# A fused linear-attention and MLP block, rewritten on a list scheduler with the output projection folded into the KV product

## The chip, the cores and the metric

The kernel runs on one core of a Trainium2 chip. The metric is device time in microseconds (us). Several executions of each kernel are timed, and kernels that are compared ran on the same chip beside fresh executions of the kernel before. Each execution also lists its span, which is the length that the trace shows, and the mean clock that the throttle granted to TensorE. An execution that lies more than 1.5% above the fastest of its kernel is called slow.

PE is TensorE's matmul pipe, PEld its weight loads, DVE is VectorE, ACT is ScalarE, POOL is GpSimd, SP is the engine that issues most loads.

## The reference, cut to what matters

```python
S, D, F, H = 2048, 448, 1792, 16              # Dh = 28, bfloat16
xn  = layernorm(x)
q, k, v = split(xn @ wqkv)                    # 3 x 448 columns
phi = lambda t: where(t > 0, t + 1, exp(t)) + 1e-6
kv  = einsum("bhsd,bhse->bhde", phi(k), v);  z = phi(k).sum(over s)
o   = (phi(q) @ kv) / (phi(q) . z + 1e-6)     # per head
s   = o @ wo
g   = silu(relu(xn @ w1 + b1) ** 2 @ w2 + b2)
out = x + s * g
```

The 2048 tokens are 16 tiles of 128, handled as four groups of four tiles. D = 448 is contracted in four chunks of 112 rows, in both kernels.

## The kernel before

It is written engine by engine, with semaphores set by hand. For each group it emits K, V and Q per tile, then the 14 blocks of W1. After the last group come the KV product, the denominators, and a phase that interleaves W2 with the attention output. Here are the parts that the change and the argument touch.

The start: 64 dummy matmuls, the transposes of group 0, 24 more dummies, then K and V. The bias b1 comes in a column layout, element by element, from GpSimd's queue.

```python
emit("pe", pe_prewarm(64))
for piece in ln_pieces(0):
    for fpc in piece:
        emit("dve", fpc)
emit("pe", pe_transposes(0))
emit("pe", pe_prewarm(24))
# ... in GpSimd's setup:
with nc.allow_non_contiguous_dma(reason="b1 column layout"):
    e.dma_start(b1f[:, :], B_b1.rearrange("(fi p) -> p fi", p=P)).then_inc(s_b1, 16)
# ... on SP: x as four single tiles, then the weights
for j in range(min(4, NT)):
    e.dma_start(x_tok[:, j : j + 1, :], x_r[:, j : j + 1, :]).then_inc(s_x0[j], 16)
e.dma_start(w_qkv[:PD, :, :], A_wqkv.rearrange("(c p) j -> p c j", p=PD)).then_inc(s_wqkv, 16)
```

The denominators (16 matmuls, each using 16 columns of the array), the 16 spreads of 1/den over the rows of a head, and the 16 numerator steps:

```python
# pe_denhs(ni), for each of four groups:
for c in range(NC_D):
    last = e.matmul(DHps[ni][:NH, 0:512], zind[:PD, c, :], pqT[:PD, c, ni * 512 : (ni + 1) * 512],
                    start=(c == 0), stop=(c == NC_D - 1))
# pe_rdb(w), one bank per (group, chunk):
e.matmul(RBps[w % 2][:PD, 0:512], ehead[:NH, c, :], r16[:NH, ni * 512 : (ni + 1) * 512], start=True, stop=True)
# pe_numT(w):
e.matmul(OBps[w % 2][:PD, 0:512], kvbd[:PD, c, :], pqT[:PD, c, ni * 512 : (ni + 1) * 512], start=True, stop=True)
# ... ScalarE copies it to xoT; pe_s(si) multiplies it with w_o, four matmuls per tile
```

## Time and profile before

| | us |
|---|---|
| time, median of three | 183.68 (183.58 to 183.89) |
| span of the profiled execution | 183.8 |
| first K matmul | 11.51 |
| W1 of group 0 begins | 21.03 |
| group 1 begins | 37.25 |
| denominators end, first W2 tile begins | 113.21 |
| last W2 tile ends, after it the last four matmuls | 177.9, 178.7 |

These lines are from the profile page of the kernel before: the busy time of the engines with its share of the span, the granted TensorE clock in 40 slices (in tenths), and the chain of waits by engine and by line.

```profile
PE 171.7 (93%) x968; PEld 89.5 (49%) x968; DVE 126.0 (69%) x294; ACT 96.8 (53%) x156; POOL 27.2 (15%) x42
...
PEclk9999999999999999999999999999999999999997
...
PE 75%; DMA 10%; DVE 7%; POOL 2%; issue 2%; ACT 1%; POOLq 0%; DVEq 0%; ACTq 0%
PE pb L715 24%; PE pb L549 19%; DMA b1f<-in_B_b_dram 10%; PE pb L757 6%; PE pb L468 6%; PE pb L438 5%; PE pb L450 5%; PE pb L667 3%; PE pb L691 2%; PE pb L633 2%; DVE r2hT L573 2%; PE pb L597 2%; DVE xn_tok L342 2%; PE pb L401 1%; ACT ra L5
```

PE is busy for 93% of the span, so only matmuls that go away, or a shorter start and tail, can save much. The load of b1 is 10% of the chain. Next, PE's timeline of the kernel before. The columns are start and length in us, engine and line, operation and operands with their shape, count, and in brackets the idle time just before and what ended it.

```profile
1.59 6.37 PE L824 MATMUL pb<-ident 128*128 128x128 bf16 x64 [1.59 <-POOL eps L218]
...
8.75 1.50 PE L824 MATMUL pb<-ident 128*128 128x128 bf16 x24
11.51 0.93 PE L438 MATMUL pb<-w_qkv,xoT 112*128 112x448 bf16 x4 [1.26 <-DMA w_qkv<-in_A_wqkv_dram]
...
21.03 3.62 PE L549 MATMUL pb<-xoT,w 112*128 112x512 bf16 x16
26.00 6.20 PE L549 MATMUL pb<-xoT,w 112*128 112x512 bf16 x28 [1.35 <-ACT ra L563]
...
109.66 3.62 PE L633 MATMUL pb<-pqT,zind 112*16 112x512 bf16 x16 [0.44 <-DVE zind L611]
...
121.83 0.38 PE L691 MATMUL pb<-pqT,kvbd 112*112 112x512 bf16 x1
122.14 0.42 PE L667 MATMUL pb<-r_50,ehead 16*112 16x512 bf16 x1
122.50 2.82 PE L715 MATMUL pb<-w,r2hT 128*128 128x448 bf16 x14
```

K waits for its weights. In the first W1 stage PE stops for 1.35 us on ScalarE's relu, which itself waits for b1: that load takes 19 us. The lines from 109.66 to 122.14 us are the small attention matmuls. A spread costs a slot of 0.36 us (122.14 to the next matmul at 122.50), a numerator 0.31, and the denominators 3.62 us together.

### The profile page before, as it was taken

Reading aid. Unit: us, or ns where it says so; the run is one execution under the profiler, and the core shown is the slowest. Engines: PE = TensorE matmul, PEld = TensorE weight load, DVE = VectorE, ACT = ScalarE, POOL = GpSimd, SP = SyncE. Lnnn points to the kernel's source line nnn. Section 1 sums busy time; section 2 is a strip of 40 time slices with the busy share of each in tenths; the row PEclk is TensorE's granted clock in tenths of the full one; section 3 lists DMA queues with packets and bytes.
Section 4 is the critical chain, followed back from the end, with each engine's and each line's share of the span. In section 5 each row is a group of like instructions: output and inputs, shape, how many; then the busy total and the mean of one; then the engine's idle time right before and its main releaser. Section 6 shows DMA issues by size and latency. Waiting matters only on the chain.

```text
span 183.8 us, 2904 instructions
## 1 busy us (share of the span) xinstructions
PE 171.7 (93%) x968; PEld 89.5 (49%) x968; DVE 126.0 (69%) x294; ACT 96.8 (53%) x156; POOL 27.2 (15%) x42
## 2 busy tenths in 40 slices
PE   6979979799998999989999999999999999999980
PEld 6945424455444554445544474444444444434540
DVE  3727959969999699996995440194665556587454
ACT  6447557477784777748778747932332222352120
POOL 7500000000000000000000000000015544468320
PEclk9999999999999999999999999999999999999997
DMA  5999990000000000000000000000000000112101
GB/s 119 258 264 230 253 334 21 0 5 0 0 0 4 0 0 0 2 4 0 0 0 4 2 0 4 0 0 0 0 0 29 27 25 30 45 50 79 50 26 49
DMA packets 9629, 8.78 MB, mean 48 GB/s; under 512 B 2256, under 2 KB 8720, under 8 KB 9616
## 3 DMA queue, kind: packets, MB, share of 16 engines
q1 hardware_dynamic: 7808, 8.60, 17.4%
q0 software_dynamic: 1808, 0.01, 1.4%
q8 instruction: 8, 0.13, 0.3%
q14 instruction: 5, 0.04, 0.1%
HBM read 6.77 MB, written 1.84 MB: 47 GB/s over the span
## 4 chain that ended last, share of the span: by engine, by line
PE 75%; DMA 10%; DVE 7%; POOL 2%; issue 2%; ACT 1%; POOLq 0%; DVEq 0%; ACTq 0%
PE pb L715 24%; PE pb L549 19%; DMA b1f<-in_B_b_dram 10%; PE pb L757 6%; PE pb L468 6%; PE pb L438 5%; PE pb L450 5%; PE pb L667 3%; PE pb L691 2%; PE pb L633 2%; DVE r2hT L573 2%; PE pb L597 2%; DVE xn_tok L342 2%; PE pb L401 1%; ACT ra L563 1%
## 5 line engine op out<-in xcount | busy, mean ns | idle before, releaser
L549 PE MATMUL pb<-xoT,w 112*128 112x512 bf16 x224 | 49.7, 379 | 1.4 <-ACT ra L563 1.4
L563 ACT ACTIVATE ra<-pb,b1f 128x512 bf16<-128x512 f32 x56 | 37.7, 688 | 19.0 <-PE pb L549 14.6
L715 PE MATMUL pb<-w,r2hT 128*128 128x448 bf16 x224 | 45.0, 353 | 0.0
L800 POOL TENSOR_TENSOR outb<-tt_52,x_tok 128x448 bf16<-128x448 f32 x15 | 21.2, 1417 | 149.6 <-DVE tt_52 L788 149.6
L549 PEld LDWEIGHTS pb<-xoT,w 112*128 112x128 bf16 x224 | 21.7, 98 | 27.2 <-issue 1.8
L715 PEld LDWEIGHTS pb<-w,r2hT 128*128 128x128 bf16 x224 | 20.9, 98 | 21.4 <-issue 3.1
L737 ACT ACTIVATE sgm_54<-gb_53 128x448 bf16<-128x448 bf16 x16 | 9.2, 576 | 39.9 <-DVE gb_53 L728 39.9
L573 DVE TENSOR_TENSOR r2hT<-ra 128x512 bf16<-128x512 bf16 x56 | 22.0, 422 | 8.6 <-ACT ra L563 8.6
L728 DVE TENSOR_TENSOR gb_53<-pb,b2b 128x448 bf16<-128x448 f32 x16 | 10.0, 624 | 23.3 <-PE pb L715 23.3
L468 PE MATMUL pb<-xoT,w_qkv 112*112 112x512 bf16 x64 | 16.4, 379 | 0.0
L438 PE MATMUL pb<-w_qkv,xoT 112*128 112x448 bf16 x64 | 14.7, 353 | 1.3 <-DMA w_qkv<-in_A_wqkv_dram 1.3
L450 PE MATMUL pb<-w_qkv,xoT 112*128 112x448 bf16 x64 | 14.7, 352 | 0.0
L757 PE MATMUL pb<-w_o,xoT 112*128 112x448 bf16 x64 | 14.7, 352 | 0.0
L503 DVE TENSOR_SCALAR rt_q<-pb 112x512 bf16<-112x512 f32 x16 | 11.1, 691 | 4.2 <-ACT e_q L487 4.2
L768 DVE TENSOR_TENSOR gg_51<-gb_53,sgm_54 128x448 f32<-128x448 bf16 x16 | 10.0, 624 | 4.7 <-ACT sgm_54 L737 4.6
L788 DVE TENSOR_TENSOR tt_52<-pb,gg_51 128x448 f32<-128x448 f32 x16 | 10.0, 625 | 4.2 <-PE pb L757 3.8
L494 DVE TENSOR_SCALAR rt_k<-pb 128x448 bf16<-128x448 f32 x16 | 10.0, 625 | 3.9 <-ACT e_k L479 3.3
L487 ACT ACTIVATE e_q<-pb 112x512 bf16<-112x512 f32 x16 | 9.6, 597 | 5.1 <-PE pb L468 5.1
L479 ACT ACTIVATE e_k<-pb 128x448 bf16<-128x448 f32 x16 | 8.7, 544 | 4.4 <-PE pb L438 4.4
L517 DVE SCALAR_TENSOR_TENSOR pqT<-e_q,rt_q 112x512 bf16<-112x512 bf16 x16 | 11.0, 685 | 0.0
L699 ACT ACTIVATE xoT<-pb 112x512 bf16<-112x512 f32 x16 | 9.3, 585 | 3.0 <-PE pb L691 3.0
L468 PEld LDWEIGHTS pb<-xoT,w_qkv 112*112 112x112 bf16 x64 | 8.3, 130 | 5.2
(65 smaller groups left out, 153.6 us busy)
## 6 DMA issues: line engine op xcount, KB each, us to landing
w<-in_B_w_dram SPq DMA_DIRECT2D x2, 1568.0 KB, 15.8
out_dram<-outb SPq DMA_DIRECT2D x16, 112.0 KB, 1.7
x_tok<-in_A_x_dram SPq DMA_DIRECT2D x3, 448.0 KB, 17.4
w_qkv<-in_A_wqkv_dram SPq DMA_DIRECT2D x1, 1176.0 KB, 8.8
x_tok<-in_A_x_dram SPq DMA_DIRECT2D x4, 112.0 KB, 2.1
w_o<-in_A_wo_dram SPq DMA_DIRECT2D x1, 392.0 KB, 19.8
b2b<-in_B_b_dram SPq DMA_DIRECT2D x1, 112.0 KB, 13.5
b1f<-in_B_b_dram POOLq DMA_DIRECT2D x1, 7.0 KB, 19.0
```

The costliest lines, as they stand in the source:

```text
L438: last = e.matmul(Kps[:, 0:D], xoT[:PD, c, si * 128 : (si + 1) * 128], w_qkv[:PD, c, QW : QW + D], start=(c == 0), stop=(c == NC_D - 1),)
L450: last = e.matmul(Vps[:, 0:D], xoT[:PD, c, si * 128 : (si + 1) * 128], w_qkv[:PD, c, VW : VW + D], start=(c == 0), stop=(c == NC_D - 1),)
L468: last = e.matmul(Qps[t % 2][:PD, 0:512], w_qkv[:PD, c, m * PD : (m + 1) * PD], xoT[:PD, c, g * 512 : (g + 1) * 512], start=(c == 0), stop ...
L494: e.tensor_scalar(out=rt_k[:, si % 2, :], in0=Kps[:, 0:D], scalar1=0.0, scalar2=1e-6, op0=ALU.max, op1=ALU.add,).then_inc(sv_rtk, 1)
L503: e.tensor_scalar(out=rt_q[:PD, t % 2, :], in0=Qps[t % 2][:PD, 0:512], scalar1=0.0, scalar2=1e-6, op0=ALU.max, op1=ALU.add,).then_inc(sv_r ...
L517: e.scalar_tensor_tensor(out=pqT[:PD, m, g * 512 : (g + 1) * 512], in0=e_q[:PD, t % 2, :], scalar=1.0, in1=rt_q[:PD, t % 2, :], op0=ALU.mi ...
L549: last = e.matmul(pb[bk][:, 0:512], w_1[:PD, c, fi * 128 : (fi + 1) * 128], xoT[:PD, c, g * 512 : (g + 1) * 512], start=(c == 0), stop=(c ...
L563: e.activation(out=ra[:, u % NRB, :], in_=pb[h_bank(fi)][:, 0:512], func=AF.Relu, bias=b1f[:, fi : fi + 1],).then_inc(sa_hr, 1)
L573: e.tensor_tensor(out=r2hT[:, fi, g * 512 : (g + 1) * 512], in0=ra[:, u % NRB, :], in1=ra[:, u % NRB, :], op=ALU.mult,).then_inc(sv_sq, 1)
L715: last = e.matmul(Gps[si % NGD][:, 0:D], r2hT[:, fi, si * 128 : (si + 1) * 128], w_2[:, fi, :], start=(fi == 0), stop=(fi == NF - 1),)
L757: last = e.matmul(Sps[si % 2][:, 0:D], xoT[:PD, c, si * 128 : (si + 1) * 128], w_o[:PD, c, :], start=(c == 0), stop=(c == NC_D - 1),)
L800: e.tensor_tensor(out=outb[:, si % 3, :], in0=tt[:, si % 2, :], in1=x_tok[:, si, :], op=ALU.add,).then_inc(sm_, 1)
```

## The change

The intent: describe the work as operations with reads and writes, let a list scheduler with assumed durations fix the order of each engine (the orders of PE and of the load queue stay as written), and shorten PE's stream on the way. The core of the diff is this:

```diff
-        emit("pe", pe_prewarm(64))
-        emit("pe", pe_transposes(0))
-        emit("pe", pe_prewarm(24))
+        warm(40)
+        pe_transpose([0])
...  (group 0: one transpose and one K/V pair per tile, in turn)
+                kv(0)
+                for si in range(1, 4):
+                    pe_transpose([si])
+                    kv(si)
...  (loads)
-            for j in range(min(4, NT)):
-                e.dma_start(x_tok[:, j : j + 1, :], x_r[:, j : j + 1, :]).then_inc(s_x0[j], 16)
+        load_x(0, 1)
+        load_k("act", w_qkv, A_wqkv, "wqkv", 3 * D)
+        load_x(1, 4)
+        dma("sp", b1r[:, :], B_b1.rearrange("(f p) -> f p", p=P), ["b1r"], F * 2)
...  (Wo folded into the masked KV block; z comes out of the same bank)
-                e.matmul(OBps[w % 2][:PD, 0:512], kvbd[:PD, c, :], pqT[...], start=True, stop=True)
+                e.matmul(ps(b)[0:PD, 0:D], kvm[0:PD, c, :], w_o[0:PD, c, :], start=True, stop=True)
+                return e.matmul(ps(b)[0:PD, D : D + 32], kvm[0:KA, c, :], zsel[0:KA, c, :], start=True, stop=True)
...  (denominators: group g in columns 32g to 32g+31 of one bank)
+                for c in range(4):
+                    for g in range(NG):
+                        last = e.matmul(
+                            ps(denb)[32 * g : 32 * g + 32, 0:512], msb[0:PD, c, D : D + 32],
+                            pqT[0:PD, c, g * 512 : (g + 1) * 512], start=(c == 0), stop=(c == 3),
+                        )
...  (spread: four groups from four 32-row strips)
+                for g in range(NG):
+                    r = slice(32 * g, 32 * g + 32)
+                    last = e.matmul(ps(bufs[g])[0:PD, 0:512], ehd[r, c, :], rden[r, :], start=True, stop=True)
```

The rest of the diff: phi is computed in place, the gate is one Silu in place of Sigmoid and a multiplication, 1/sqrt comes from a power on GpSimd, and b1 arrives as 14 rows that PE transposes. A constant `SPLIT64` could lay the fourth chunk out as two 64-row halves that run side by side; it is `False`, so 4 x 112 rows remain.

## The prediction

> **What bounds it now.** The 183.68 us are a TensorE stream. In the chain of waits PE holds 75%, and from about 34 us it is unbroken. The chain's timeline gives the issue spacing: 0.216 us per 512-column matmul (W1: 12 in 2.59 us), 0.189 per 448-column one (4 in 0.756). Summed over K, V, Q, W1, W2, Wo, the transposes and the small attention matmuls, that is about 162 us of the 166.4 between the first QKV matmul (11.51 us, waiting for w_qkv) and the last (177.9). Lost outside the stream: 11.5 us of start; about 3.5 us in the first W1 stage (24.65 to 26.0 idle for b1, which lands at 25.17, then transposes waiting for VectorE); 5.8 us of tail.
>
> **What goes.** (1) The numerator matmuls disappear because Wo is folded into KV: 16 steps of 0.22 to 0.35 us, about 4.0. (2) Denominators (16 matmuls, 3.62 us) go to four 32-column groups, and the 1/den spreads (16 steps of 0.35, and each makes the next W2 run 0.10 longer: 2.75 against 2.65 us, together about 7 us) to four 32-row groups. The build gives them distinct array tiles. The Trainium skill ("TensorE: Matmul & The Clock Gate", Part 3) reports about 3x for four row tiles at once; no trace here shows it yet. Estimate: 1.0 us and 4 x 0.6. (3) The b1 wait. (4) Sigmoid times gate (10 us of VectorE): off the critical path. (5) The tail: one VectorE multiply, one SBUF add of about 0.4 us each for two tiles, then the store: about 4.0.
>
> **What comes.** Four fold steps, about 1.0 us. After the denominators Ln, a table load (1.28 us in the trace) and Exp no longer hide behind two W2 tiles, only one: about 1.1 us of PE idle.
>
> PE stream: 162 - 4.0 - 2.6 - 4.6 + 1.0 = about 152 us.
>
> **The start gets worse, I think.** w_qkv now shares the DMA engines with x from a second queue; the same bytes moved at about 260 GB/s in the old trace, so it lands near 11.3 us as before. Only 40 warm-up matmuls run (to about 6 us), so the first K/V probably run at half clock (same page, Part 1). And the static VectorE order puts the statistics of x tile 8 before the evacuation of transposed tile 3. Those x tiles landed at 21.6 us in the old trace, after the same 4.2 MB; I expect about 20. So PE stalls 2 to 3 us before tile 3's K/V. W1 of group 0 starts near 26 us (before: 21.0), group 1 near 39 (before: 37.4).
>
> **Sum.** 39 + two groups of 23.2 + last group with fold and denominators 24.8 = 110.3 (old end of denominators: 113.3). Then 16 W2 tiles x 2.65, 16 output tiles x 0.756, spreads 2.4, idle 1.1, small losses 0.3: 168.3. Tail 4.0: about 172 us, 6.4% less. Range 168 to 176.5.
>
> **Right or wrong, step by step.** Den group about 1 us and each spread about 0.6 in the timeline, else add up to 5 us. PE idle before the first spread naming ScalarE. VectorE waiting for the x load in the first 22 us, with PE idle behind it. Groups 1 and 2 at 23 us each with no PE idle over 0.3 us. W2 at 2.65 us throughout.
>
> **What would break it.** Row or column groups running one after another (175 to 177). A static order that makes PE wait for VectorE in every group. A faster x load (168 to 169).

## The result, and the profile after

| | before | after |
|---|---|---|
| time, median | 183.78 (183.58 to 184.96, 4 executions) | 176.69 (174.86 to 178.96, 4 executions) |
| span of the profiled execution | 183.8 | 177.2 (a slow one, 178.96 us) |
| W1 of group 0 begins | 21.03 | 30.75 |
| group 1 begins | 37.25 | 44.59 |
| groups 1 and 2, each | 23.45, 23.44 | 23.35, 23.34 |
| first W2 tile begins | 113.21 | 115.75 |
| first W2 tile to the end of the last matmul | 65.5 | 57.6 |

The ratio is 0.9555 (95% interval 0.9481 to 0.9629), so the kernel is faster by 4.5%. A ratio here is the mean time of one kernel's fast runs over that of the other's in the same rounds, so not quite the ratio of the medians. The profiled execution of the kernel after was a slow one, and so was that of e0_after, so no fast execution of this kernel has a trace.

The same parts of the page, for the kernel after:

```profile
PE 162.2 (92%) x913; PEld 85.5 (48%) x913; DVE 102.6 (58%) x240; ACT 83.3 (47%) x131; POOL 25.0 (14%) x42
...
PEclk9955569999999999999999999999999999999998
...
PE 87%; DMA 5%; ACT 4%; DVE 2%; issue 0%; SPq 0%; DVEq 0%
PE pb L604 27%; PE pb L725 23%; PE pb L570 17%; PE pb L590 8%; PE pb L749 7%; DMA x_tok<-in_A_x_dram 5%; PE pb L475 2%; PE pb L635 2%; DVE st L412 1%; PE pb L704 1%; ACT L693 1%; ACT L689 1%; ACT xT L488 1%; DVE xT L487 0%; PE pb L658 0%; A
```

PE's busy time fell by 9.5 us, and b1 is gone from the chain. In its place stand the load of x with 5%, K/V (L570) with 17% where the two lines of before had 10% together (in part because the chain of before passes group 0 through the b1 load), and a clock row with fives in slices 3 to 5. PE's timeline of the kernel after, start and then the end of the groups:

```profile
1.60 4.04 PE L786 MATMUL pb<-ident 128*128 128x128 bf16 x40 [1.60 <-POOL eps L325]
11.89 0.68 PE L475 MATMUL pb<-ident,xn 128*112 128x128 bf16 x4 [6.25 <-DVE xn L441]
...
13.26 3.17 PE L570 MATMUL pb<-w_qkv,xT 112*128 112x448 bf16 x8 [0.57 <-ACT xT L488]
...
17.54 3.17 PE L570 MATMUL pb<-w_qkv,xT 112*128 112x448 bf16 x8 [0.70 <-ACT xT L488]
...
25.77 1.69 PE L570 MATMUL pb<-w_qkv,xT 112*128 112x448 bf16 x8 [0.52 <-DVE xT L487]
...
30.75 5.34 PE L604 MATMUL pb<-xT,w 112*128 112x512 bf16 x24
...
114.77 1.05 PE L677 MATMUL pb<-pqT,msb 112*32 112x512 bf16 x16
115.75 2.82 PE L725 MATMUL pb<-w,r 128*128 128x448 bf16 x14
119.56 0.43 PE L704 MATMUL pb<-rden,ehd 32*112 32x512 bf16 x4 [0.99 <-ACT rden L693]
119.92 2.82 PE L725 MATMUL pb<-w,r 128*128 128x448 bf16 x14
```

The end is what was hoped for: 16 denominator matmuls in 1.05 us in place of 3.62, four spreads in one slot of 0.36 us. The start is not. PE stands idle for 6.25 us after only 40 dummies, and then a K/V pair of eight matmuls takes 3.17 us, three times over, before it takes 1.69. DVE's timeline of the kernel after shows what PE waited for:

```profile
4.55 0.63 DVE L412 BATCH_NORM_STATS2 st<-x_tok 128x6 f32<-128x448 bf16 x1 [4.55 <-DMA x_tok<-in_A_x_dram]
...
9.67 1.68 DVE L412 BATCH_NORM_STATS2 st<-x_tok 128x6 f32<-128x448 bf16 x3 [4.09 <-DMA x_tok<-in_A_x_dram]
11.26 0.14 DVE L432 SCALAR_TENSOR_TENSOR nmr<-mv,rstd 128x1 f32<-128x1 f32 x1
...
11.44 0.40 DVE L441 TENSOR_SCALAR xn<-x_tok,rstd,nmr 128x448 bf16<-128x448 bf16 x1
```

Tile 0 landed at 4.55 us, but its normalisation at 11.44 stands behind the statistics of tiles 1 to 3, whose load landed at about 9.6. The scheduler had assumed an earlier load. On a static order, a late load delays work that does not need it. That load took 8.4 us, while the K/V weights moved on a second queue. With those weights behind x on one queue it took 4.3 us (experiment e5_start). This agrees with the Trainium skill ("DMA: Bandwidth & Descriptors", "Queues, rings and completion order"): each DMA engine takes turns between the queues that have work for it.

### The profile page after: what moved, and what is told of

It is laid out like the page before. It is cut to its first block, busy times and chain, and to the rows that moved or that the text cites. A ratio compares the mean times of both kernels' runs of the same rounds, so it can differ in the third digit from the quotient of the medians.

```text
span 177.2 us, 2340 instructions
## 1 busy us (share of the span) xinstructions
PE 162.2 (92%) x913; PEld 85.5 (48%) x913; DVE 102.6 (58%) x240; ACT 83.3 (47%) x131; POOL 25.0 (14%) x42
## 4 chain that ended last, share of the span: by engine, by line
PE 87%; DMA 5%; ACT 4%; DVE 2%; issue 0%; SPq 0%; DVEq 0%
PE pb L604 27%; PE pb L725 23%; PE pb L570 17%; PE pb L590 8%; PE pb L749 7%; DMA x_tok<-in_A_x_dram 5%; PE pb L475 2%; PE pb L635 2%; DVE st L412 1%; PE pb L704 1%; ACT L693 1%; ACT L689 1%; ACT xT L488 1%; DVE xT L487 0%; PE pb L658 0%; ACT lnd L689 0%
## 5 line engine op out<-in xcount | busy, mean ns | idle before, releaser
L604 PE MATMUL pb<-xT,w 112*128 112x512 bf16 x224 | 50.8, 379 | 0.0
L615 ACT ACTIVATE r<-pb,b1f 128x512 bf16<-128x512 f32 x56 | 38.5, 687 | 16.4 <-PE pb L604 16.4
L725 PE MATMUL pb<-w,r 128*128 128x448 bf16 x224 | 44.9, 353 | 0.0
L623 DVE TENSOR_TENSOR r<-r 128x512 bf16<-128x512 bf16 x56 | 23.2, 422 | 17.6 <-ACT r L615 17.6
L604 PEld LDWEIGHTS pb<-xT,w 112*128 112x128 bf16 x224 | 21.4, 98 | 23.8
L570 PE MATMUL pb<-w_qkv,xT 112*128 112x448 bf16 x128 | 29.8, 395 | 2.3 <-ACT xT L488 1.3
L725 PEld LDWEIGHTS pb<-w,r 128*128 128x128 bf16 x224 | 21.5, 98 | 20.9 <-issue 1.3
L763 POOL TENSOR_TENSOR obuf<-obuf,x_tok 128x448 bf16<-128x448 bf16 x14 | 14.3, 1032 | 120.1 <-DVE obuf L758 120.1
L570 PEld LDWEIGHTS pb<-w_qkv,xT 112*128 112x128 bf16 x128 | 13.2, 106 | 16.4 <-issue 4.0
L590 PE MATMUL pb<-xT,w_qkv 112*112 112x512 bf16 x64 | 15.0, 379 | 0.0
L749 PE MATMUL pb<-msb,pqT 112*128 112x448 bf16 x64 | 13.9, 352 | 0.0
```

The lines of the kernel that those rows point to most:

```text
L570: return e.matmul(ps((kb, vb)[w])[:, 0:D], xT[rows, c, si * P : (si + 1) * P], w_qkv[rows, c, col : col + D], start=start, stop=stop,)
L590: return e.matmul(ps(bufs[w])[0:PD, 0:512], w_qkv[rows, c, col : col + PD], xT[rows, c, g * 512 : (g + 1) * 512], start=start, stop=stop,)
L604: return e.matmul(ps(bufs[w])[:, 0:512], w_1[rows, c, col : col + P], xT[rows, c, g * 512 : (g + 1) * 512], start=start, stop=stop,)
L615: lambda e, _, fi=fi, slot=slot, buf=bufs[w]: e.activation(out=slot, in_=ps(buf)[:, 0:512], func=AF.Relu, bias=b1f[:, fi : fi + 1]),
L623: return e.tensor_tensor(out=slot, in0=slot, in1=slot, op=ALU.mult)
L725: last = e.matmul(ps(b)[:, 0:D], r2[:, fi, si * P : (si + 1) * P], w_2[:, fi, :], start=(fi == 0), stop=(fi == NF - 1),)
```

## The experiments

Where DVE's order was changed by hand, the program was emitted in topological order in place of the simulated start times, so that every wait is still derived. All kernels gave a correct result. W1 stands for the start of W1 in group 0, read from PE's timeline. The expectations count it a little later (0.15 us), from the chain of waits.

### e0_after: the kernel after again, unchanged

> The changed kernel itself, once more, so that the others have it on the same chip. Both theories: 174.5 to 179 us, mean granted clock between 0.94 and 0.98, differing from run to run.

Measured: 177.18 us median (176.28 to 179.73), ratio 0.9608 (0.955 to 0.9665). The result repeats, and so does its spread of over 3 us. Granted clocks were 0.942 (slow), 0.999, 0.995 and 0.999. In the profiled execution, the slow one, four K/V pairs ran at 3.17 us and Q took longer (3.93 us for 16 matmuls, else 3.62).

### e1_warm: 145 dummies, the same order

```diff
-            add("pe", f, ["ident"], [b], n * 0.1)
+            add("pe", f, ["ident"], [b], 40 * 0.1)
...
-        warm(40)
+        warm(145)
```

The first pair of lines keeps the scheduler's assumed duration at that of 40 dummies, so that no order changes.

> The changed kernel with 145 instead of 40 warm-up matmuls and nothing else; no engine's order changes. They fill the time in which PE waits for the first transposed tile (5.6 to 11.9 us). Theory A (the first three K/V blocks ran at half clock because PE stood idle after the warm-up): the blocks take 1.55 us each and not 3.17, W1 of group 0 starts near 26.2 us and not 30.9, the time is near 172.5 us, the mean clock at least 0.99, and the runs agree within 0.5 us. Theory B (the start is held by data, that is by loads and VectorE, and the half clock only fills waits): W1 starts at 29 us or later and the time stays above 175.

Measured: 174.23 us (174.19 to 174.35), ratio 0.9465 (0.9428 to 0.9501). The span was 172.5 us, which is the number that was expected; I had written a span down as a time. PE's timeline:

```profile
1.59 10.91 PE L786 MATMUL pb<-ident 128*128 128x128 bf16 x145 [1.59 <-POOL eps L325]
...
13.41 1.69 PE L570 MATMUL pb<-w_qkv,xT 112*128 112x448 bf16 x8 [0.58 <-ACT xT L488]
...
26.06 4.26 PE L604 MATMUL pb<-xT,w 112*128 112x512 bf16 x19
```

The first K starts 0.15 us later than in the kernel after, and W1 begins 4.7 us earlier. Every K/V pair takes 1.69 us. The three cold pairs account for 3 x 1.48 = 4.4 us of it and the transposes for most of the rest. The spread between executions falls from 3.45 us (e0_after, same batch; 1.48 us among its fast ones) to 0.16 us. So the cold clock, and not the loads, set the spread and the time by which the two kernels differ. In kind it agrees with the Trainium skill ("TensorE: Matmul & The Clock Gate", Part 1): the array starts at half rate, about 3.4 us of sustained work releases it, and an idle window of about the same length takes it back. The starts of the dummies give the figures: 0.107 us apart at first, 0.056 us once the clock is released. The release came 2.9 to 5.7 us after the first dummy, in 12 of the 14 traces. In the kernel after it came after 3.5 us, for the last few dummies alone; then 6.25 us of idle left the array cold.

### e2_before_40: the kernel before with 40 dummies

```diff
-        emit("pe", pe_prewarm(64))
+        emit("pe", pe_prewarm(40))
...
-        emit("pe", pe_prewarm(24))
```

> The kernel before with the warm-up of the changed one: 40 matmuls in place of 64, and the 24 after the transposes left out. Theory A: its first K, V and Q blocks then run at half clock too (0.37 us per matmul and not 0.19), the mean clock falls to 0.96 to 0.98, the time rises by 2 to 5 us to 186 to 189, and the runs spread by more than 1 us. Theory B: within 0.5 us of before, as the loads decide the start.

Measured: 184.91 us (184.17 to 187.32), ratio 1.003 (0.998 to 1.0081). The first K, V and Q ran cold: 1.65, 1.70 and 1.21 us in place of 0.93, 0.92 and 1.03. W1 began at 21.98, 0.95 us later than in the profile before. The expected 186 to 189 was too much. The trace, which is that of the fastest of the four executions, shows two things. All 40 dummies start 0.107 us apart, so the clock was never released by them; it came back during the first Q, some 3 us after the first K, in a stretch of K, V and Q without idle. In the kernel after, idles of 0.52 to 0.70 us stand between the cold pairs; that they prolong the cold state is likely, but not shown. And this execution had no b1 wait: the b1 load took 14.7 us in place of 19.0 and had landed before W1, so W1 ran unbroken and group 1 began at 35.9 us.

### e4_order: tile 0 normalised ahead of the statistics of tiles 1 to 3

```diff
         pr.schedule()
+        d = pr.order["dve"]
+        early = [d[i] for i in (0, 1, 2, 6, 8, 3, 4, 5, 7, 9, 10, 12, 15, 17, 19, 21)]
+        pr.order["dve"] = early + [o for o in d if o not in early]
```

> The changed kernel with one change of VectorE's order: tile 0 is normalised as soon as its statistics are there, and tiles 1 to 3 before the statistics of tiles 4 to 6; in the changed kernel the statistics of tiles 1 to 3, whose load lands at 9.64 us, stand ahead of tile 0's normalisation. Both theories: the first K/V starts when w_qkv has landed, near 9.4 us and not 13.3. Theory A: the first blocks still run at half clock, so only 2 to 2.5 us of the 3.9 remain: 174 to 175.5 us beside a changed kernel of 176.7. Theory B: nearly all of the 3.9 us remains, 173 or less.

Measured: 174.42 us (173.09 to 175.71), ratio 0.945 (0.9379 to 0.9521), within theory A's 174 to 175.5. PE's timeline of the profiled execution, a fast one:

```profile
1.59 4.45 PE L804 MATMUL pb<-ident 128*128 128x128 bf16 x40 [1.59 <-POOL eps L343]
...
9.27 3.17 PE L588 MATMUL pb<-w_qkv,xT 112*128 112x448 bf16 x8
...
17.95 1.69 PE L588 MATMUL pb<-w_qkv,xT 112*128 112x448 bf16 x8 [0.52 <-DVE xT L505]
...
25.35 1.89 PE L622 MATMUL pb<-xT,w 112*128 112x512 bf16 x8
```

The first K came at 9.27 us (13.26 in the kernel after), although it is cold: two pairs at 3.17 us, then 1.69, W1 at 25.35. The load of tiles 1 to 3 was about as slow as before (7.5 us), so the order of DVE alone cost about 4 us of start; of these, 2.9 us show in the time (mean of the fast executions 173.98, in e0_after 176.88). The 40 dummies took 4.45 us and again start 0.107 us apart to the last: here, too, they did not release the clock, so it was cold from the beginning and not through an idle. The page of this execution gives a granted clock of 0.999 although two pairs ran at half speed; the note at the end comes back to it.

### e5_start: warm, in order, and one load queue

The order of e4_order, 75 dummies plus 16 in front of K, all four transposes before K, the K/V weights behind x on SP's queue, and the statistics of tiles 8 to 11 moved behind the first Q.

```diff
-        warm(40)
-        pe_transpose([0])
+        warm(75)
+        for si in range(4):
+            pe_transpose([si])
...
+                warm(16)
...
+        w = next(o for o in pr.order["act"] if o.nbytes)   # the load of w_qkv
+        pr.order["act"].remove(w); w.eng = "sp"; pr.order["sp"].insert(2, w)
```

> The changed kernel with its start rearranged and nothing else: w_qkv behind x tiles 0 to 3 in one load queue, VectorE normalises tiles 0 to 3 before any other statistics and takes those of tiles 8 to 11 after the Q of group 0, PE transposes all four tiles before the first K/V, 75 + 16 warm-up matmuls. Theory A (all that the prediction missed inside the span lay in the start: half clock, tile 0 waiting for tiles 1 to 3, and one wait for the evacuation of each tile): K/V starts near 10.5 us, W1 of group 0 near 20 us and not 26.2 (with the long warm-up alone) or 30.9, time 168 to 168.5 us. Theory B (the loads, w1 above all, hold W1 back): W1 not before 23 us, time above 171.

Measured: 171.2 us (171.16 to 172.82), ratio 0.9311 (0.9238 to 0.9383). Better than either single step, yet W1 began at 22.98 and not at 20. PE's timeline names the cause:

```profile
11.49 1.04 PE L493 MATMUL pb<-ident,xn 128*112 128x128 bf16 x12 [2.65 <-DVE xn L459]
```

Tiles 1 to 3 had landed long before. Their normalisation came at 11.04 because the power for tile 0 stood behind GpSimd's constants until 6.2 us, DVE waited for it, and everything else queued behind. By its numbers (W1 at 22.98 us, 171.2 us) this stands at the threshold of theory B, but the loads, B's cause, did not hold the start.

### e6_start_g1: two W2 tiles ahead of the first spread

```diff
         gg(0)
-        spread(0)
         gg(1)
+        spread(0)
```

> As the kernel with the rearranged start, and two W2 tiles instead of one between the denominators and the first 1/den spread. PE stood idle there for 1.0 us waiting for ScalarE (table load, Ln, table load, Exp). If that idle time is a loss, this takes 1.0 us less than the rearranged start alone, near 167.2 us; if VectorE's scaling only moves and holds the output matmuls later, less than 0.4 us.

Measured: 171.99 us (170.35 to 172.0), ratio 0.9303 (0.9241 to 0.9365). The median is no better than that of e5_start, because in the profiled execution the first K/V pairs were cold again (a group's K/V in 7.30 us in place of 6.06), after 3.15 us of idle where e5_start had 2.65; two more executions have the same time and clock (172.0 us, 0.988 and 0.989), so probably the same start. Read from the stage it touches, the step works: the first spread follows W2 at 115.05 us with no idle, and from W1 to the end of the span it takes 145.6 us in place of 146.4. That is 0.8 us, of the 1.0 expected, and matches the 0.99 us of idle that names ScalarE. ACT's timeline of the kernel after, which shows where that idle comes from:

```profile
115.58 1.28 ACT L689 ACT_TABLE_LOAD   x1
116.88 0.69 ACT L689 ACTIVATE lnd<-pb,eps 128x512 f32<-128x512 f32 x1
117.58 1.28 ACT L693 ACT_TABLE_LOAD   x1
118.88 0.63 ACT L693 ACTIVATE rden<-lnd 128x512 bf16<-128x512 f32 x1
```

### e7_den_serial: the denominators group by group

```diff
-                for c in range(4):
-                    for g in range(NG):
+                for g in range(NG):
+                    for c in range(4):
```

> The changed kernel with the long warm-up (174.2 us), and the 16 denominator matmuls in another order: the four of one 32-column group one after another, so that neighbours no longer lie in different column groups. Theory A (the groups overlap only because neighbours alternate): they take 3.4 to 3.6 us in place of 1.05, and the time rises by about 1.5 us to 175.7, as PE's 1.0 us wait for ScalarE takes up the rest. Rival (a matmul with 32 output columns is short by itself): 1.05 us still, no change.

Measured with one look (state unknown): 173.88 us, and the denominators in 1.08 us. PE's timeline:

```profile
109.69 1.08 PE L677 MATMUL pb<-pqT,msb 112*32 112x512 bf16 x16
```

My theory that neighbouring matmuls have to alternate between column groups falls: with four matmuls of one group in a row it is just as short, as the rival expected. What is shown is that 16 matmuls spread over four column groups take 1.05 to 1.08 us in either order, and that 16 in one column group took 3.62 us in the kernel before. In both orders they start in four bursts of four, about 0.216 us apart; in the kernel before they start singly, 0.216 us apart. Those were 16 columns wide, and no run puts matmuls of 32 columns into one group alone, so the rival as a cause is not tested. How the array overlaps four that accumulate in the same group is left open.

### e8_split64: the 64-row layout, on e1_warm

```diff
-SPLIT64 = False
+SPLIT64 = True
```

> The changed kernel with the long warm-up, and the contraction of 448 as 3 x 128 + 64 in place of 4 x 112, by the switch that the changed kernel holds but leaves off: the two 64-row remainders of a pair of tiles lie in different row groups. Theory A (the halves overlap): per pair 7 matmul times in place of 8, 10.8 us less over 52 pairs, less about 0.24 us for each of 26 visits to the half-array mode (the spreads' cost): 169 to 171 us. Rival (the halves run one after another and each switch costs): 178 us or more.

Measured: 170.5 us (169.99 to 171.12), ratio 0.9245 (0.9191 to 0.93), so 3.7 us less than e1_warm by the medians, 4 us by the ratios (the two ran on different chips). From the start of a W1 stretch of 24 matmuls to the next work it takes 4.73 to 4.86 us in place of 5.18, and K/V of a later group 5.72 in place of 6.05. It is less than a full eighth, and around the matmuls of 64 rows PE's weight load stands idle for up to 0.42 us. With `SPLIT64` off, the change left this gain unused.

### e9_before_b1: the kernel before with the kernel after's bias load

```diff
-                e.dma_start(b1f[:, :], B_b1.rearrange("(fi p) -> p fi", p=P)).then_inc(s_b1, 16)
+            e.dma_start(b1r[:, :], B_b1.rearrange("(fi p) -> fi p", p=P)).then_inc(s_b1r, 16)
...
+            e.transpose(b1ps, b1r[:, :], ident[0:NF, 0:NF]).then_inc(st_b1, 1)
...
+            e.tensor_copy(b1f[:, :], b1ps).then_inc(s_b1, 1)
```

> The kernel before with one thing changed: the bias b1 comes as 14 rows on the queue of x and is transposed by PE, as the kernel after does it, in place of the load of 1792 elements of two bytes each. Theory (the b1 wait is a real cost of the kernel before, as its profile shows 1.35 us of PE idle and 10% of the chain): 1.3 to 2 us faster, 182 us. Rival (the wait was there only in the profiled execution, as in e2_before_40, where W1 ran without it): less than 0.5 us.

Measured: 181.87 us (181.52 to 182.13), ratio 0.9894 (0.986 to 0.9929), so 2 us faster; that is clear of noise, but under 2%. The first W1 stage runs unbroken. The first K also came at 10.04 us in place of 11.51, still waiting for its weights. Whether the element-wise load also delayed the weights is not settled: in e2_before_40 the first K came at 10.87 us with that load still there.

### e10_start2 and e11_best: the start once more, and all gains together

e10_start2 normalises tiles 0 to 3 together with one power ahead of GpSimd's last constants, and uses 100 dummies and 8 more, with the K/V weights behind x on SP's queue. It also puts the normalisation of tiles 4 to 7 behind the first Q, and that of tiles 8 to 15 in one block after a transposed pair of group 1. e11_best adds the two W2 tiles of e6 and the layout of e8.

```diff
+        rest[a:a] = groups[1]      # a: after the last phi(Q) of group 0
+        rest[b:b] = groups[2]      # b: after the second transposed pair of group 1; tiles 8 to 15
```

> The start once more, with what the trace of e5_start showed to be in the way taken out: tiles 0 to 3 are normalised together (one pow of four columns on Pool, ahead of Pool's last constants), the K/V weights follow the first x tiles on one queue, 100 warm-up matmuls reach to about 8 us, and eight more bridge to the first K. Theory (order of work on VectorE and Pool and a cold clock held the start): first K near 10.9 us, when its weights have landed, at full clock; W1 of group 0 near 20.4 us (e5_start: 23.1); time 168 to 169 us. Rival (the x and weight loads hold it): W1 still at 22.5 us or later, PE idle in front of it naming a load, 170.5 us or more.

> The start of e10_start2, two W2 tiles ahead of the first spread (e6_start_g1: -0.8 us) and the 64-row layout of the contraction (e8_split64: -3.7 us). If the three gains are independent, the time is that of e10_start2 less 4.5 us: about 164 us. If the 64-row layout and the early start compete for VectorE and ScalarE (four twin copies more in the start, a ScalarE near its limit in W1), less than 3 us of it is seen: 165.5 or more.

Measured: e10_start2 177.79 us (176.21 to 178.2), ratio 0.9654 (0.9598 to 0.9711), verdict "unclear"; e11_best 174.3 us (173.56 to 175.03), ratio 0.9481 (0.9447 to 0.9514). Both are far slower than the theories said; the rivals' open ranges hold the times, but not for the rivals' reasons. The start is as planned (K at 11.29 and 11.91 us, W1 at 21.02 and 21.58), but PE's timeline of e10_start2 has this in group 1:

```profile
46.03 4.66 PE L588 MATMUL pb<-w_qkv,xT 112*128 112x448 bf16 x12 [5.50 <-DVE pqT L577]
```

The block of eight normalisations stood ahead of phi(Q) of group 1 on DVE, so PSUM was not read and PE stopped for 5.5 us. After that idle its clock was cold again: 12 matmuls in 4.66 us, and a granted clock of 0.974 to 0.980 in all ten executions. The early start was bought with a new wait, of my own making.

### e13_best2: the order mended

The tiles of each group are normalised right after the last phi(Q) of the group before, and GpSimd's last constants come after the second power.

```diff
-        rest[b:b] = groups[2]
+        for g in (1, 2, 3):
+            i = [i for i, o in enumerate(rest) if o.writes[0] == ("pq", g - 1, 3)][1] + 1
+            rest[i:i] = groups[g]
```

> e11_best with its VectorE order mended. The traces of e10_start2 and e11_best show the start as planned (K at 11.3 and 11.9 us, W1 of group 0 at 21.0 and 21.6) and then a PE idle of 5.5 and 5.9 us in the K/V of group 1: the normalisation of tiles 8 to 15, which those two kernels put in one block in front of the phi of group 1, stands in VectorE's way. Here the tiles of each group are normalised right after the last phi of the group before, and Pool's last constants come after the second pow. Theory (that block alone cost the time): K near 11.4 us, W1 of group 0 near 21 us, no PE idle over 0.3 us in groups 1 to 3, W1 of group 1 near 43.3 (e11_best: 51.9); time near 165 us, between 164 and 166. Rival (an early start only moves the wait: VectorE and ScalarE cannot keep up when PE begins 5 us earlier): PE idle of over 1 us turns up elsewhere and the time is 167 or more.

Measured: 166.64 us (166.04 to 167.59, six executions), ratio 0.9058 (0.9027 to 0.9089). It beats both kernels: 9.4% faster than before, about 10 us below the kernel after. The loss of e11_best lay in that stage: W1 of group 1 begins at 44.07 us in place of 51.92, and the medians differ by 7.7 us. GpSimd's constants were moved in the same run; their share is not separated. The time is 0.6 us above the expected range. PE's timeline shows three waits that are left:

```profile
11.66 1.59 PE L588 MATMUL pb<-w_qkv,xT 128*128 128x448 bf16 x8 [0.83 <-DMA w_qkv<-in_A_wqkv_dram]
...
21.11 5.02 PE L622 MATMUL pb<-xT,w 128*128 128x512 bf16 x24
...
30.82 0.61 PE L493 MATMUL pb<-ident,xn 128*128 128x128 bf16 x8 [0.36 <-DVE xn L473]
...
58.38 1.86 PE L608 MATMUL pb<-xT,w_qkv 128*112 128x512 bf16 x8 [0.87 <-DVE xT L505]
```

The load of the K/V weights is now the first limit. The expectation of no idle over 0.3 us was wrong twice, with idles of 0.36 and 0.87 us: DVE reaches xn and the copies of xT late. The trace shows what goes with the wait of 0.36 us. The four normalisations took 2.12 us here and 1.31 us in e11_best, and here GpSimd builds its constants at the same time (28.13 to 31.41 us). That agrees with the Trainium skill ("SBUF — State Buffer", "SBUF: two separate sides"): DVE and GpSimd share a port pair that one of them locks. No run shows the lock itself.

## Why the prediction was right or wrong, point by point

The direction (faster by over 2%) was right, and so was the account of the groups and the end. The size was off: 172 us was predicted with a range of 168 to 176.5. The three fast executions lie between 174.86 and 177.03 us, their mean is 176.08, at the upper end of the range; the median, with the slow one, is 176.69. That the range holds the mean is its width's doing. The number alone would even mislead: 175 to 177 us is what the prediction gave for groups that run one after another, and the timeline shows that they overlap. What failed is the start, and a confusion of span and time.

- **Denominators "about 1.0".** 1.05 us. Right.
- **"4 x 0.6" for the spreads.** A spread takes a slot of 0.36 us, and the W2 tile behind it runs 0.10 us longer (2.75 in place of 2.65), so about 0.46. Right in kind, a little too dear. "W2 at 2.65 us throughout" held except behind the spreads.
- **Skill figure used for it.** "TensorE: Matmul & The Clock Gate", Part 3, reports about 3x for four row tiles. Here one spread took 0.36 us before and four take 0.36 now, which is about 4x; four column groups gave 3.62 / 1.05 = 3.4x.
- **PE idle of "about 1.1" naming ScalarE.** 0.99 us, and e6_start_g1 removes it. Right.
- **Groups at 23.2 us.** 23.35 and 23.34. Right.
- **Tail "about 4.0".** 3.8 us (last matmul at 173.37, span 177.2). Right.
- **The b1 wait goes.** Right, and in e9_before_b1 the other load of b1 is worth 2 us in the kernel before, not only the 1.35 us of its wait; part of it may be the earlier first K.
- **"VectorE waiting for the x load in the first 22 us, with PE idle behind it."** Seen, but for other tiles. The prediction named tile 8 and a stall in front of tile 3's K/V. The trace shows tiles 1 to 3 in front of tile 0, and the stall came before the first K.
- **"W1 of group 0 starts near 26", "group 1 near 39".** This is the step that failed: 30.75 and 44.59 us in the slow profiled execution. The prediction did say that "the first K/V probably run at half clock", but of its 5 us over the old 21.0 it named 2 to 3 as the stall of tile 8. So at most 2 to 3 us can stand for the half clock (an estimate from its figures), and three cold pairs cost 4.4 us. e1_warm puts a number to the term. With dummies alone W1 begins at 26.06 us, so the cold clock cost 4.7 us in that slow execution and 1.8 to 2.6 us between the means of the fast ones (176.08 and 176.88 in e0_after against 174.25).
- **The sum of spans was given as a time.** From group 1 on, the profiled execution took 132.6 us of span where the prediction had 133. The time is about 1.75 us more than the span. That is the second part of the miss: 172, with 1.75 for the unit and 1.8 to 2.6 for the cold clock, comes to 175.6 to 176.4. That the 26 us predicted for W1 and the 26.06 of e1_warm agree is partly luck: the stall of tile 8 that the prediction put there was not seen, and the late start of tile 0 took its place.

## What to carry to other kernels

When a rewrite changes the start, cost it as its own stage, with the clock state in it: dummies have to last until the clock is released (40 did not in two of the four traces that have 40) and to reach up to the first real matmul, because an idle of some microseconds undoes them (3.15 us did in the trace of e6_start_g1, 2.65 us in that of e5_start did not). A list scheduler's order is only as good as its load times; look on the vector engine for work that is ready and stands behind work that waits, and check after every reorder that the wait has not moved into a later group, as it did in e10_start2. And compare like with like: a sum read from the trace is a span, not the reported time.

## What the Trainium skill lacked or had wrong

- "TensorE: Matmul & The Clock Gate", Part 1: it warns that clock events in traces can be unreliable. In e4_order the mean granted clock was 0.999 and yet two K/V pairs took 3.17 us in place of 1.69. In the kernel after, the clock row starts with nines while the dummies start 0.107 us apart, against 0.056 us once released. Nor did about 3.4 us of sustained work always release the clock: in two traces 4 us of dummies did not, and in the others it took 2.9 to 5.7 us. The length of a known block tells a cold clock more safely than the column.
- "TensorE: Matmul & The Clock Gate", Part 3: its 3.07x for four row tiles was exceeded here, with about 4x (0.36 us for four spreads). For columns it has 2.38x for three tiles and no figure for four; here four column groups gave 3.4x (1.05 us for 16 matmuls). It does not say whether matmuls of one column group may follow each other; e7_den_serial shows 1.08 us in that order too.
- "TensorEngine Tiling (Array Packing)", "Key Properties", says that a change of tiling mode drains the array, but not what it costs. In e8_split64 the weight load stood idle for up to 0.42 us at a switch; what that cost PE is not separated.
- "ScalarE: Activation LUTs", "What ACT_TABLE_LOAD costs": the load of 1283 ns agrees (1.28 us), but the drain of about 1380 ns beside it does not show: Ln starts 0.02 us after the load has ended, and Exp likewise.
- "ScalarE: Activation LUTs", "Table sets": Ln followed by Exp should need one load, since one set holds both. This build loads a table for each, 1.28 us before Ln and 1.28 us before Exp.
- No page gave the time of a power on GpSimd that the kernel after uses for 1/sqrt: 0.56 us for one column, 0.88 for three and 1.01 for four.
